# K's features taken to feature rows by transfer instead of by a second transposition

## The chip, the cores and the metric

The kernel runs on one core of a Trainium2 chip. The metric is the device time of one execution in microseconds (us). A change counts here as faster or slower when it moves that time by more than 0.5%, which is about what a measurement of this kernel can tell from no change.

## The reference

Three stages, on inputs with batch 4, 8 heads, 768 positions and 48 features per head. The first is a linear recurrence per head with a complex decay, normalised to a magnitude below one:

```
for t in range(S):
    new_re = ar * S_re - ai * S_im
    new_im = ar * S_im + ai * S_re
    S_re, S_im = new_re + outer(k[t], v[t]), new_im
    y[t] = q[t] @ S_re
```

The heads are then put side by side into x (768 positions of 384 features). The second stage is a token mixer: `theta = x @ w_theta`, `y = w_tok_r @ (x cos theta) + w_tok_i @ (x sin theta)`, `u = x + y`, `u + max(u @ w_ch, 0)`. The third is a gated output: a causal convolution of five taps through a sigmoid gives a gate, and the result is `(gate * (x @ w_val)) @ w_out`.

## The kernel before

The recurrence is computed in chunks of 128 positions. The decay's cumulated logarithm and phase are turned into features: each position's q and k are multiplied by an exponential and by a cosine (tile c) and a sine (tile s), so that 48 features become 96 (a cosine half and a sine half). The score of position t against position t' is then an ordinary product of 96 features.

A granule is 256 positions of one batch, two chunks; there are 12 granules and 24 chunks. For a granule, ScalarE and VectorE make c and s. Their partitions are 16 groups of features times 8 heads, and each partition holds, for each of three features r, 256 words of q features and then 256 words of k features. The matrix products need features on partitions and heads side by side. For q this is done by six transfers per granule, the restacks (lines 616 to 622): one for each of c, s and each r, 128 rows of 256 words, from c or s into the tile st, which has 96 feature rows of 8 heads x 256 positions.

For k a chunk takes another way. TensorE transposes the k words of c and s (trans, line 652, six transpositions), ScalarE evicts them into kn, positions on partitions (kn, line 656, two instructions); TensorE transposes kn once per head, eight transpositions (back, line 660); and ScalarE evicts these into kT, features on partitions (line 663). kT is the stationary operand of the eight score products (line 668), st holds the moving one. kn is needed in any case, as the stationary operand of the state's update (line 699). VectorE masks the scores (line 672), TensorE makes the outputs from masked scores and from the carried state (yT, line 685), ScalarE evicts them (ys, line 688). After each granule the outputs go to memory and TensorE computes theta for them (line 737).

The mixer runs after this attention stage, twelve times, for three groups of 256 positions of each of four batches: the token products (tok, line 852), a first VectorE operation u (line 859), split into high and low parts (lines 792 and 793), a first dense product (line 817, ch), VectorE's o (line 871), four taps of each feature block on VectorE (line 899), a second dense product, the gate, and the output product (line 917). Its weights arrive as 8-byte numbers and are converted by VectorE (lines 419 to 421) and split (lines 489 and 490).

Every piece of work is an operation with a planned engine and duration. The order of all of them is a list written out in the file (ORDER, two characters for the number of an operation); each engine runs its operations in the order in which the list names them, and each of the two queues of transfers, SP's and POOL's, issues in that order. Where the plan sees TensorE idle for over 0.8 us, small dummy products are put in (line 1009). Loads of inputs and weights, restacks and stores are issued by SP; the loads of the mixer and of the input checks by POOL. An issue that waits holds those behind it in its queue.

Buffers: c, s, st, qk and the value tile vt exist twice and alternate by granule, ri three times. Later tiles reuse their places (PLACE): weights of the mixer lie in st0 and st1, which are also the place of kT0 and kT1. Scores, the back transpositions and theta alternate between two tiles of PSUM (A0, A1), in the order of the calls of flip (line 714).

Of the kernel before, what the change touches and what calls it, by code (L numbers as in the profile page):

```python
# [94 lines left out]
class Prog:  # L95
# [10 lines left out]
    ORDER = """  # L106
        #,#.###%#$%9#&I9#)#-#'#0#(%(#*'0#+#/%.%;#2#4%:%=#6#5#9#8#<#7#;#?#:#>#=#1#A#@#D#B#C#G#E#F#J#H#M%?#I%)#K#L$#%@#N$%%A$$'1#[$&$)%B$3$4$'%C$5%*%/
        '2%D#O%+#P#Q#R%<%H#S#U#T#V#Y#W$+#X$1#3#Z$*$($7$0$.$,$>$6%>$/$2$:$<$-$8$D'3$9$@$;'6$B%,$H'7$F%F&H$I%I$?%J$J(;$=%E$K$E$A%-$S$C'8$L$G$Q&I(<%G'9
        $U$M$R$T%0%K%1%M%L$V%N$N%#%O$W%2(A%P%Q$O&T%3%T(B$X&U$P':(C(=$Y%S(>';$Z'?%U%R(D'4'@%V$[%W(J%4%Y'5%['=&&'A'<%X%5&(%Z(E&$&#'>&')I&)%&&*%6&%)J&,
        %7%$&+'B%%&-(K'D&5&.&3%''C&7'E(F&/%8'F)O'J&63A(G&8)P&0)K&93B'G&1(H)Q)L'I&4&:(I)R&2'H&>&;(L)X'K&<'L'Q(N'O&=(O'M&C'R(M)S*X'P'W&?(P'N(R'S'Y*Y(Q  # L110
        )T'U(S&D(?(U'[&A'Z(T(#'X&@&E*Z'T(V()'V($&F(@(+)V(X(W(%&B)#+%(Z(-*[(,(*,*)U(&)+)%+&(.)))W)-)'('(/&G),+'*$(Y(0)$*%)Y)Z([3Q,++()6((+)(1)4)7)[+*
        )&(2)8)*+,++)(*#3R,0).*'*&)M*+,1(3)N)/(4(6*(,,+-)53T(5(7,2,-**&J&V&K)9*,(8+.(9)0*)+/*.+0):(:*2)?,3*0)1*/+1*3,9*1*-);+2*4,4)2*6)<+3+5*:*8*5)3
        ,5+4-8)=*7*;)@*9*<+6-9,6+9*E)>+#*=)B*G*F,7-:)D*>,:+$)C)A)E,8+8-;+7*H)F+:,;)G*?*I+;+>)H+<*C+@+?*@->+D+H+=-?+F*D+A*J+B+I-@+E,>.G+G,<-A*A+C+J*K
        .H,?-B,=-C*N*B,A-D-E-F*L-G,@,C*O+K,.,D*M+S+L*Q*T,/+U*P.I+T,E,B*R*S-H,G-I.J.M,K+V*U,I,F-J*V+M,H.N,L-K+W,Q,J+Q*W,O+N-M-N/R-L,M,S,R-P,P+R+X,U/S
        -O.O,T-S+O-Q,N-R+Y/T-%+P-T.P,V/U-'+Z-&,W-U.V-(-X+[.W.X-<,%.'-Y/X-Z-=&W-V.Q,&.#&X-).(1'-[.R/Y.%-W-#,',#.$/Z1(').S,(.T,X-$.U/[0#.).&,Y-.,$.*.Y
        &L0$.+&M'*1--*-//#.Z.[-0/$,Z-+1.,).4,[1/0%&N-,/(10.5.6.,--.K/%110&-1-41)0'.-.L&Y-3-2120,0-141*&O.2-5&P13-6...315-7/&.7/'./.=.8/)16.90(/*///+
        .0/-/0.:26/,/1/70)/..1/327.;/9/5/80/0*03/:.</V/2.@.C0+/4/;28/6/W0.00.>01/B171802.A.B/D/C29.?1904/@.D.E/<050:2<08.F062=/E/=0>0;1<0B090<2>1;07
        />0@0?/F/A0=1>1B2?0A/G0D/?0C1:2@0M/H1=0K1?2E2A/I1A2C1@1C0E/J1+0N/K/N0F1D1I1,1G0L0O1E/M2F/L2G1M1O2B1J1K1Q1H/O2DB>1F0P1R1N/P1SB;1P0G0Q1L&QB?2K
        &Z/Q&[2#2H0H0V2JB<B@'#2IBA0R0WBEB=0X2%2M&RBB0I0S2$BF2L1Z0J&SBC2P0T2O2N2Q1T0U2:BG0Y0[BH'$2;2W1UBL2R2UBD1#2S0ZBI'%2Y2[2X3C'&3&2V1$3$BM2&'+''1%
        2T1[421V2Z',2'BJ3''-3#BN3D2,1WBO49'.BS3%'(1&BK2(3UBP3F43'/3(3V1X2)4:3G313W443)1Y453HBT2*2-BQ32332.3*463E4;2+5N4@BR4<2/223O3J4=4A3IBW3L4G21BU  # L120
        3KBV203XBZ34233P4&24353+4H3M3/3,BXB[3S3025363Y4$BY3ZC#4'C%C$3-373[C(4%3N6XC&3.4)38C)4#6YC'4(4*C,393:3<474+3;4-3=4,4/C-4>4.C*5A3>486Z404?3?5B
        4B4CC+6[C.5C4DC/4I3@4E4N4JC35D4K7$C0414O4U4L5E5?C15F7%C2C44F7&C64V5G4M7(4PC54Q5H5@7'C:4R5I4S5#4WC74XC;4T7#5$4YC87Y5J4Z5*C<7)7+5K4[5+C9CA5LC=
        5%5M5&7Z5'7,5,5(515-CB5OC>5)5P5Q525T5.CC5U5R58CH5/5W5VC?5X5950C@5S53CD5Y54CI5[7-55CE5:56647.5ZCJ5;CF65CO7/6%CG6#5<CK575=6=CP5>CL6$6>7066CQ6(
        67CMCV71CN6&6'CR6)72686*CW7:6?69736+CS6:6@746,6F6ACX756-6BD$6G7*6C6.768[6;6O6D6<D%8,8$CT6P6/6E608YCU6HD&CY6I8.6177629#D+6J8/786K8-6M6Q796R6L
        8Z6S9%CZ6N6V636T806WD,6U7;819&7[7@7=7A827<7>9,7D8#7C7B7FC[7G7?7ID#7E7J9'D'7H7L9(7K837ND-7MD(8%9-D2847O8;9)7P85D3D)8&7Q868'7R8)7S878(8+92D*94
        8*D4D.7U9.7T93;*D99/D/9$8895;+:'7V7W9+D0D:96D19*7XD589;-97D;:(;.:)908:D@D6;/91:*;1DAD798D88<:,D<8@99:-DB8A8=D=DG9:8>8C8?8F:.8D9;D>8GDH8E;08I
        9<8HD?8K:0DC8L8B:/9=8J9>:3DD8N8MDI9?8ODN:4:+DE8P9A:5DF;(:18QDODJ:68R;):2DP8SDUDK8T<*8UDVDLDM9@<+8VDQ8WDWE#8X<-:79BDR<.9C9GE$:89D9H9EDS:99JE%
        9M</E*9P;,9S<19K::<(DT9N;3E+9FDX<0:;9Q9L<)9OE,9I9RDYE19U9T;29V:BDZ>2E2D[:<9WE&9X>3:=E39YE'E8<,:>9[=/<3:?E9>5;4:@9ZE(=0<2:$E):A>6:#;5E-E::%>7
        =1>8:&E;>9E<;6:CE.=2:D:H;7:E:IE=E/;8E0:K:N:FE4:G:LE>;9:ME?:O<4:QEDE5:R;::P:U=4<5:JEEE6E7=5E@EF:T=6:SEG:V;;:WELEA=8:X;<;C<6EM;=EB<7:YEN;>EO:Z
        ECET=7=3;?EH;#<8=:EU>0;@<9:[EI<:;%EV>1<<=9EWF#EJ;A;$<;EK<=;&EPF$;B?2;'F%EQF&?3F+<>;DERES;FEXF,<?;H;L;O;E?5<@;R;KEYF-?6F.<A;GF3;I?7;NEZ;JE[;Q  # L130
        ;M?9F4F';P?8;T;S;VF5F(;UF6>4<I;WF;<B>:F)?0;XF*<CF<F/>;;Y?1<D;ZF=F>F0<#<EFC<F=;==<%<GF1FDF2=>F7=<FE;[FFF8FK<H<$<&F9FLF:<'F?FM=?<JFNF@<K<OFS=@
        <L<P<M=AFA<RFTFB<S<N<UFG<T=B<WFU<ZFV<QFH=$F[<V<Y=#<XFIG#FJ<[=%FO=C=&=JG$=DG%FP='G*=(=EFQG+FR?4=FFW=)?:=G><G,=H=*G-FX=+G2?;>==I=,FY=-FZG3G&=.
        G4>>=KG5G'G:=P>?=L=M=Q=O=NG;>@=UG(=SG)=XG.=T>A=WG<=VG=?<=YGB>B=ZG/=[>%>C?=GCG0G1>D?>>#G6>$>E>KGD??GEG7>&GJ=RG8GKG9G>>F>'GLGMG?>(GRA0>G?@>)?B
        ?D>HGS?AG@>*GA?CGF>IGTGU>+>,GZGG>J>->.G[GHGI>/GNH#H$?E>LH)>PGO?F>M>Q>NH*>O?G>TGP>SGQ>VGV?H>YH+>UH,>XH1?I>[GW?%>W?#>RAQH2>ZARAP?$GXAO?QGYH3H%
        H4AN?JH9?&H&?'?K?(H:?)?LH'H(H-H;?+H<?MHA?NH.A3@7?-?OHB?*H/@8H0H5?P?,HC?.HDHIH6?/@9?RH7HJ?S?W@:?T?X?VH8@;?Z?UH=@#HK@$HL?[@<@&HQ@)H>@%@=@,@'HR
        @(@+@>H?@*H@@-@FHE@?HSHTHY?YHFHZHGHHHM@@@.H[I#@/I(@AHN@0A6@BI)HO@CA,@2HP@DI*HUI+@1A-@4I0HV@E@3@5I1HW@6HXI$I2A.I3@G@H@LA8A/I%@J@MA;@KA1@P@I@Q
        I&@OI'@T@N@SI,@W@R@Z@UI-@V@X@YA2A<@[AAI.A#I/A4I4A$A5A%I5A&A7A9A'A:A(I6I7A=I8A)A*A?A+A>ABA@AFACAGAHASAIADAEATAXAUAJAYB'AVAZAWALA[B#AKB%B$B&B)
        AMB+B*B(B/B,B-B0B.B1B3B2B5B4B6I:B8I;B9B7B:
    """
# [158 lines left out]
class Kernel:  # L298
# [893 lines left out]
```

## Time and profile before

| | |
|---|---|
| time, median of 3 runs | 544.9 us (543.25 to 546.31) |
| the profiled execution: its own time | 542.7 us |
| its span, first to last instruction | 541.0 us |
| busy: TensorE matmul, weight load, VectorE, ScalarE, GpSimd | 521.0, 476.8, 427.8, 428.1, 91.7 us |
| moved by transfers | 97.70 MB |

PE is TensorE's matmul, PEld its weight load, DVE VectorE, ACT ScalarE, POOL GpSimd, SP the engine that issues most transfers. PEclk is the clock that TensorE was granted, 1.00 being the upper of its two levels. DMA is the mean busy share of the 16 transfer engines. The matmul's ends are modelled, so a busy PE is not a PE at its peak. The stages in time: attention from 0 to about 240 us, the mixer from 240 us to the end.

### The profile page before, as it was taken

What the parts mean: (1) busy time and instruction counts of PE and PEld (TensorE: products, weight loads), DVE (VectorE), ACT (ScalarE), POOL (GpSimd) and SP (SyncE); (2) the same over time, 40 slices, a digit from 0 to 9 for tenths busy, and PEclk for the clock granted to TensorE, in tenths of its full rate; (3) what the DMA queues carried; (4) which work ended last, traced back from release to release, by engine and by line L of the source; (5) the groups of instructions that cost most, each with busy time, mean ns of one, the idle gap of its engine ahead of it and who ended that gap; (6) DMA issues with size and microseconds to landing.
All of it is one profiled execution on the core that took longest, in us unless ns stands there. A gap on an engine that the chain in (4) does not pass through costs nothing.

```text
span 541.0 us, 12968 instructions
## 1 busy us (share of the span) xinstructions
PE 521.0 (96%) x5298; PEld 476.8 (88%) x5298; DVE 427.8 (79%) x589; ACT 428.1 (79%) x790; POOL 91.7 (17%) x185
## 2 busy tenths in 40 slices
PE   8998999999999999999899999999999999999995
PEld 3586797889888898879799999999999999999994
DVE  6999999999999999689899979567683674644552
ACT  7998999999996998986559988778676576664552
POOL 2002000000000011122222233331322222122100
PEclk9999999999999999999899999999999999999998
DMA  8659595867948579748668264453534334233311
GB/s 346 222 182 246 160 294 185 265 210 212 311 166 266 134 196 301 258 147 301 227 216 281 63 205 129 155 179 95 176 118 137 115 101 139 81 118 88 119 44 36
DMA packets 36629, 97.70 MB, mean 181 GB/s; under 512 B 5056, under 2 KB 20432, under 8 KB 36560
## 3 DMA queue, kind: packets, MB, share of 16 engines
q1 hardware_dynamic: 26992, 62.15, 36.5%
q0 software_dynamic: 9568, 34.63, 20.7%
q8 instruction: 43, 0.70, 0.6%
q14 instruction: 26, 0.21, 0.1%
HBM read 73.17 MB, written 14.16 MB: 161 GB/s over the span
## 4 chain that ended last, share of the span: by engine, by line
PE 63%; ACT 14%; DVE 9%; DMA 9%; issue 3%; POOL 0%; SPq 0%; ACTq 0%; POOLq 0%; DVEq 0%
PE A L852 23%; PE A L817 14%; PE Y L917 6%; DMA ri<-in_aT 5%; PE A L668 4%; PE Y L685 4%; PE A L737 4%; ACT L990 2%; PE Y L699 2%; PE A L660 2%; PE X L652 1%; PE X L760 1%; DVE c L604 1%; DMA wraw<-in_wtok 1%; ACT ri L597 1%
## 5 line engine op out<-in xcount | busy, mean ns | idle before, releaser
L899 DVE SCALAR_TENSOR_TENSOR masks<-vt,small,masks 128x256 f32<-128x256 f32 x140 | 60.8, 481 | 2.0 <-ACT masks L882 0.7
L439 ACT ACTIVATE masks<-masks,cst 128x192 f32<-128x192 f32 (+2 forms) x105 | 56.0, 534 | 6.5 <-DMA masks<-in_aT 4.4
L737 PE MATMUL A<-wth,ys 128*128 128x384 f32 x144 | 49.1, 489 | 0.0
L871 DVE SCALAR_TENSOR_TENSOR vt<-A,vt 128x768 f32<-128x768 f32 (+1 forms) x12 | 11.2, 935 | 40.3 <-PE A L817 40.3
L452 POOL DMA_DIRECT2D masks<-in_aT x48 | 26.3, 548 | 87.8 <-ACT masks L439 73.6
L737 PEld LDWEIGHTS A<-wth,ys 128*128 128x128 f32 x144 | 26.3, 190 | 15.6 <-issue 0.2
L817 PE MATMUL A<-st,shch 128*128 128x256 f32 x210 | 32.7, 290 | 3.2 <-ACT st L792 2.3
L685 PE MATMUL Y<-sT,vt 128*32 128x128 f32 x768 | 33.4, 275 | 1.7 <-ACT ys L688 1.0
L431 ACT ACTIVATE masks<-masks 128x192 f32<-128x192 f32 (+1 forms) x57 | 21.1, 369 | 16.3 <-DMA masks<-in_wtok 9.4
L672 DVE TENSOR_TENSOR sT<-A,xt 128x1024 f32<-128x1024 f32 x24 | 29.2, 1217 | 5.7 <-PE A L668 5.5
L817 PE MATMUL A<-sT,kn 128*128 128x256 f32 x210 | 33.3, 284 | 0.0
L817 PEld LDWEIGHTS A<-st,shch 128*128 128x128 f32 x210 | 29.2, 197 | 3.8 <-ACT st L792 2.4
L586 POOL COPY small<-ri 128x3 f32<-128x3 f32 x12 | 5.5, 461 | 158.7 <-DVE ri L577 96.6
L990 ACT ACT_TABLE_LOAD x23 | 29.5, 1283 | 1.2 <-PEq L1181 0.8
L699 PEld LDWEIGHTS Y<-vt,kn 128*96 128x96 f32 x320 | 29.2, 165 | 1.1 <-issue 0.7
L699 PE MATMUL Y<-vt,kn 128*96 128x48 f32 x320 | 30.1, 247 | 0.0
L817 PEld LDWEIGHTS A<-sT,kn 128*128 128x128 f32 x210 | 28.8, 192 | 0.1
L685 PE MATMUL Y<-st,kn 96*32 96x128 f32 x640 | 28.7, 272 | 0.0
L660 PE MATMUL A<-ident,kn 128*96 128x128 f32 x192 | 25.3, 275 | 3.3 <-ACT kn L656 3.3
L917 PE MATMUL Y<-sT,wtmp 128*128 128x384 f32 x120 | 27.1, 339 | 0.0
L660 PEld LDWEIGHTS A<-ident,kn 128*96 128x96 f32 x192 | 20.8, 126 | 6.9 <-ACT kn L656 4.2
L463 POOL DMA_DIRECT2D masks<-in_wtok x32 | 17.2, 537 | 48.0 <-ACT masks L439 24.2
(231 smaller groups left out, 1654.4 us busy)
## 6 DMA issues: line engine op xcount, KB each, us to landing
qk<-in_qkT SPq DMA_DIRECT2D x12, 768.0 KB, 5.9
wraw<-in_wtok SPq DMA_DIRECT2D x12, 768.0 KB, 5.3
masks<-in_aT POOLq DMA_DIRECT2D x48, 192.0 KB, 3.4
ri<-in_aT SPq DMA_DIRECT2D x11, 768.0 KB, 5.7
masks<-in_wtok POOLq DMA_DIRECT2D x32, 192.0 KB, 2.6
vt<-in_v SPq DMA_DIRECT2D x12, 448.0 KB, 4.4
st<-c SPq DMA_DIRECT2D x36, 128.0 KB, 3.8
st<-s SPq DMA_DIRECT2D x36, 128.0 KB, 4.2
```

The source lines that it names most:

```text
L439: self.act(n, lambda: self.nc.scalar.activation(x(), x(), AF.Relu, scale=scale, bias=self.bias(j), accum_out=out()), [b], [b, (self.accb, ...
L452: self.dma("POOL", P * PIECE * 4, lambda x=x, s=src[:, a, c : c + PIECE]: nc.gpsimd.dma_start(x(), s), [], [x], name="ld check")
L660: nc.tensor.transpose(kq()[0:K2, h, :], kn()[:, h].rearrange("p z e -> p (z e)"), self.ident)
L672: self.dve(H * C, lambda: ve.tensor_tensor(sT(), sc(), cm(), op=ALU.mult), [sc, self.causal], [sT], name="mask")
L685: mm(y()[32 * c : 32 * c + 32, blk, :], x[:, at : at + 32], rhs, start=n == 0, stop=n == len(todo) - 1, tile_position=(0, 32 * c))
L699: mm(su()[:, col(h) : col(h) + D], kn()[:, h].rearrange("p z e -> p (z e)"), v(h), start=True, stop=True)
L737: nc.tensor.matmul(th()[:, i, 0:DM], xt()[:, r, i * P : (i + 1) * P], w()[:, r * DM : (r + 1) * DM], start=r == 0, stop=r == R - 1)
L817: nc.tensor.matmul(block(j), w[a]()[:, r * DM + j * P : r * DM + (j + 1) * P], x[c]()[:, r, :], start=first, stop=i == len(todo) - 1 and R ...
L852: nc.tensor.matmul(block(j), z[x]()[:, i, a, j * P : (j + 1) * P], wts[i][y]()[:, o : o + TG], start=first, stop=final)
L899: self.dve(TG, lambda k=k, r=r: ve.scalar_tensor_tensor(gt()[:, r], o()[:, r, k : k + TG], wk(k, r), gt()[:, r], op0=ALU.mult, op1=ALU.add ...
L917: nc.tensor.matmul(ot[i]()[:, 0:DM], gp[a]()[:, r, i * P : (i + 1) * P], w[c]()[:, r * DM : (r + 1) * DM], start=n == 0 and 0 in rs, stop= ...
L990: self.nc.scalar.preload_act_table_set(o)
```

## The change

k's features are restacked together with q's: a restack now moves 128 rows of 512 words (256 of q, then 256 of k), and a row of st is 8 heads x 512 words. The score product takes k from st. The back transpositions, their eviction and the tiles kT0 and kT1 are gone; trans and kn stay. An operation fewer on TensorE and on ScalarE per chunk changes all later numbers, and the list of the order is written anew as a whole: of 2191 numbers 2143 are left. flip is called once less per chunk, so the scores of successive chunks alternate between the two PSUM tiles.

```diff
-    wh10=("c1", 0), ..., ha=("st0", 3072), kT0=("st0", 2048), kT1=("st1", 2048),
+    wh10=("c1", 0), ..., ha=("st0", 3072), 
...
     ORDER = """
...
-        st = self.sb(f"st{p2}", [K2, H, L])
+        st = self.sb(f"st{p2}", [K2, H, 2 * L])
...
-            q.dma_start(rows, x()[:, r, 0:L])
+            q.dma_start(rows, x()[:, r])
...
-                self.dma("SP", P * L * 4, ..., [(x, (0, r))], [(st, (half, r))], name="restack")
+                self.dma("SP", P * 2 * L * 4, ..., [(x, (0, r)), (x, (1, r))], [(st, (half, r))], name="restack")
...
-        k = lambda h: kT()[:, h]
+        k = lambda h: st()[:, h, L + j * C : L + (j + 1) * C]
...
-        kn, kT = self.sb(f"kn{ci % 2}", [P, H, 2, D]), self.sb(f"kT{ci % 2}", [K2, H, C])
-        kq = self.ps(f"A{self.flip()}", [P, H, C])
+        kn = self.sb(f"kn{ci % 2}", [P, H, 2, D])
...
-        def back():
-            for h in range(H):
-                nc.tensor.transpose(kq()[0:K2, h, :], kn()[:, h].rearrange("p z e -> p (z e)"), self.ident)
-
-        self.pe(0.88, back, [kn], [kq], name="back")
-        self.act(H * C, lambda: act(kT(), kq()[0:K2], AF.Copy), [kq], [kT], psum=1, name="kT")
...
-        self.pe(1.79, scores, [st, kT], [sc], name="scores")
+        self.pe(1.79, scores, [st], [sc], name="scores")
```

What the two lists say, read engine by engine with the operations' names: VectorE has 246 operations ahead of the last mask in the old list and 240 in the new. Ahead of the second mix's u it has 314 in both, and they are the same 314 operations. TensorE has, apart from the 24 back groups, the same operations ahead of the second mix's first dense product in both. Between a granule's last feature and the mask of its first chunk the old list has 9 to 26 VectorE operations, the new one 11 to 16 (granules 2 to 12). On SP the new list issues the first load of w_theta ahead of the first load of q and k.

## Rows read from the trace of the kernel before

**Rows 1.** Busy time by stretch: stretch, length, PE, PEld, DVE, ACT, POOL, clock, DMA.

```profile
0.00:20.00 20.00, 18.57 (x73) 7.89 (x74) 14.90 (x43) 16.41 (x37) 2.91 (x13) 1.00 0.86 341
20.00:237.00 217.00, 209.12 (x2731) 179.43 (x2730) 205.65 (x237) 202.58 (x297) 17.19 (x32) 1.00 0.73 221
237.00:287.60 50.60, 47.94 (x556) 45.60 (x554) 44.90 (x64) 33.52 (x63) 10.76 (x19) 0.97 0.70 225
287.60:541.00 253.40, 245.38 (x1942) 243.89 (x1941) 162.33 (x248) 175.59 (x396) 60.86 (x121) 0.99 0.40 124
...
40.00:60.00 20.00, 17.50 (x239) 15.40 (x241) 19.31 (x23) 18.42 (x26) 3.38 (x2) 1.00 0.71 200
60.00:80.00 20.00, 18.35 (x227) 15.53 (x220) 19.05 (x22) 19.93 (x30) 1.39 (x2) 1.00 0.96 263
```

**Rows 2.** Chain of waits, attention stage: start, us, what; first and last of a kind.

```profile
31.33 0.91 ACT st L663
...
137.22 1.01 ACT st L663
...
150.41 1.01 PE A L660 x8
...
224.62 0.87 PE A L660 x8
225.52 2.05 PE A L668 x16
```

**Rows 3.** Who VectorE waited for, 0 to 287.6 us: total, times, longest.

```profile
DVE sT L672 <- PE A L668: 5.5, 5, 4.0
DVE ri L547 <- ACT gt L545: 4.2, 4, 3.0
DVE ri L771 <- ACT ri L768: 2.5, 2, 2.2
DVE c L604 <- ACT ri L597: 1.6, 3, 0.6
DVE st L793 <- ACT st L792: 1.4, 1, 1.4
```

**Rows 4.** Instructions in order of time, start of the second mix: VectorE, then TensorE.

```profile
287.66 0.94 DVE L859 TENSOR_TENSOR vt<-A,ev 128x768 f32<-128x768 f32 x1
...
294.05 0.62 PE L817 MATMUL A<-st,shch 128*128 128x256 f32 x3 [0.59 <-DVE st L793]
```

**Rows 5.** Groups by line: what is removed, back and kT; count, busy, mean ns.

```profile
L660 PE MATMUL A<-ident,kn 128*96 128x128 f32 x192 | 25.3, 275 | 3.3 <-ACT kn L656 3.3
L663 ACT ACTIVATE st<-A 96x1024 f32<-96x1024 f32 x24 | 24.3, 1012 | 0.7 <-PE A L660 0.5
```

**Rows 6.** Transfers, 20 to 237 us: total, then issues, KB each, median us to landing.

```profile
DMA packets 21519, 47.98 MB, mean 221 GB/s; under 512 B 2528, under 2 KB 14304, under 8 KB 21488
...
qk<-in_qkT SPq DMA_DIRECT2D x9, 768.0 KB, 5.4
st<-c SPq DMA_DIRECT2D x36, 128.0 KB, 3.8
st<-s SPq DMA_DIRECT2D x36, 128.0 KB, 4.2
xT<-ys SPq DMA_DIRECT2D x12, 384.0 KB, 4.3
```

**Rows 7.** All restacks (line 618): time from issue to landing.

```profile
DMA to landing us min/median/max: 2.3/4.1/8.7
```

**Rows 8.** Instructions in order of time: SP, TensorE and VectorE, single places.

```profile
2.19 0.43 SPq L520 DMA_DIRECT2D qk<-in_qkT  x1
...
206.49 1.84 SPq L618 DMA_DIRECT2D st<-s  x3
...
5.45 1.09 DVE L547 TENSOR_TENSOR ri<-gt,ri 128x256 f32<-128x256 f32 x3 [3.05 <-ACT gt L545]
...
12.05 1.89 DVE L599 TENSOR_TENSOR s<-s,qk 128x512 f32<-128x512 f32 x3
...
253.94 3.08 PE L1009 MATMUL A<-ident 128*128 128x64 bf16 x100
```

More of the change, by code (lines that the diff above doesn't have):

```diff
@@ L64 @@
     zh0=("qk0", 0), zl0=("qk1", 0), zh1=("gt0", 0), zl1=("gt1", 0),
-    wh10=("c1", 0), wl10=("s1", 0), wh11=("st0", 0), wl11=("st0", 1536), ha=("st0", 3072), kT0=("st0", 2048), kT1=("st1", 2048),
+    wh10=("c1", 0), wl10=("s1", 0), wh11=("st0", 0), wl11=("st0", 1536), ha=("st0", 3072),
     wh20=("st1", 0), wl20=("st1", 1536), la=("st1", 3072), wh21=("c0", 0), wl21=("s0", 0),
@@ L106 @@
     ORDER = """
[L107 to L136, printed above, removed]
@@ L137 @@
-        I&@OI'@T@N@SI,@W@R@Z@UI-@V@X@YA2A<@[AAI.A#I/A4I4A$A5A%I5A&A7A9A'A:A(I6I7A=I8A)A*A?A+A>ABA@AFACAGAHASAIADAEATAXAUAJAYB'AVAZAWALA[B#AKB%B$B&B)
-        AMB+B*B(B/B,B-B0B.B1B3B2B5B4B6I:B8I;B9B7B:
+        #,#.###$#&%5#%#'#*HB#-%$#(#)#0'(#+#/%*%7#2#6%6%9#5#9#4#8#<#7#;#?#:#>#=%%#A#@#D#B#C#G#J%;#E#M#1#F#I#H#K#L%<#N$#%&#[$'%=')$$$%$)$&%'%>$5%?$4%+
+        $3%('*#O%@&@#P%D%8#S#Q#R#V%,#U#T%)#X#W#3#Y$*#Z$0$+$($,$1$6%:$-%E$.$7$<$2%B$/$>'+%F%A$8'.$:$@&A$=%C'/$D$?$A'0%G$E$;'1$9$F'2%-$B$H%I%H(/$G$J%L
@@ new lines @@
+        '3$I%K$C%J$Q%.'4(0$O'5&L$S%M$R'6$K%/$P&M%P$X%N%O$L(1$T'7%Q(2$M'=$U%W$N%S(5'8$Y$V%U%X'9(6'<%T(7%V',':$W%R(8$[%0'-(9';%[%#&$&&$Z'>(:%Y%1(>&#)9
+        '?&'&%(<&(2J'A'B&/%Z'@&-):%2(?);&1%3&0&)'C2K(;&2&.'E)?)<(='G)@&6'I'D(@%4(C(B&*'F'M'Q'O'H'S)A&+'R'K'J&3*D)B'N)C(A'Z'P&,&7(#(D&4(E'['L(F)D*E&8
+        (H(I(3'X&5)H&9&;(4)F(G*F)I(J&:&<)E)J(L*G*J(P(N'T)G&=*K&>(M($(K)M(Q)N(O)K'U(T(X&?(R(Z*L'V(Y(V(U'Y+K*M(%(S*N)(2Z)L(W'W)&)))P)*+L)O)Q)T(&)S*O+M
+        *S([2[)=)U)R('+N)'(((**T*Q)[*U)W*P)Y(+)>+Q*R+R())/3$)V*V*#(,)X)#*X(-)+*&)Z*Y+S*$(.*(*W)$+T,U),*'*Z**)%+U*%)0)-*+*[*)*,)1+V,V*3+%*H+$*1+Z+X*5
@@ new lines @@
+        *-,W*I).+&+#)2*4,X)4+[+,+(+W+**2)5,[*.)3-#+Y+-*:)6+))7-$,&++*6,%+')8-%*/,#*7+2-&+0,$.'+4+3*0+.*;,'*8+5,)+1+6,(-'.(*<+=,,,++O+;*9,**=+/-)*?.)
+        -+,-+P+?+>*@-,+<,3*>--,1-(,/.*.-+7-*..*A./-0,4*B+@-.+8,2.0,0,.+9-1*C.1+A,7,;+:,5.2,=+B,9,<,8-//..3,6-3.4-2,D,:+C,Y-4,B-7+D,E//,F+F.5/0.6-5,Z
+        +G.7&B-6.8,C+E,>-8+H/1.9+I,G&C-:,?-</4-9->+J,@/5.;,K-;/6-B,A-=-D,H/7-@-?-F.<,L08,I-C-G.:/8-E,M.=-H.A-M-A,J.+,N09,P.>0:-N/=/9.?/>,Q.@.,.B,O-I
+        /:,R0;/;.F.C0>-O.D-R-Q.H-P0?-J.N.G.J-V/<.E.L,S.I1C-K-S.O/?/A.K0@.P.M-L-W/B-T/@,T.Q.R&D-X/C&E0A/D1D/E.W/H/20B-U.S-Y0C1E&F/G.X-[0E0G/I/F/3.#.T
@@ new lines @@
+        /K/M0D-Z/J/O.Y.$.U1F1I.%0H0F/Q.[.Z/U1J/#/S0I.V/L0M0L/N/W/$0J/P/X&N.&/%/Y0K&O0N/R0'1K/&0</V/'/)0(0O&G/T1L0S0)0=1M/*0P/(1N0R&H/Z/+0T1R/,0*0Q/[
+        0V/-0X0U0%0Z1O0W0#0Y0&0+1#0[0.1%0$1P1'&P1$1S1)1Q1&&Q&Z0,1+1(1*&[1T1W121X1G1,0/1UAD&I0-1HAG14000103131V&S&JAE1Y1Z022$042#AH1[&T2%1005AF06151-
+        AI2'AKAJ2)072&AN2+1.2(112-2LAL162/231/2*2119&R252,24AM'#AO&KAR172.&U2M'$AP2<184W&V201<1>2='%2>222O1:3BAS&W'&2N1=3%1?&X3;2X3CAQ1;2PATAU261@&Y
+        AY3<2Q1A''3&2:272Y2?3D2;2R3EAV2S2T1B283'2U3(AZ2@3/3#292V3=3-2A3)306(A[3>AW3*3.B'2B3?2C2E3+3F3I6)2W3PAX322D31B#2F333@B(3G3,3J344J353A363Q4K37
@@ new lines @@
+        2G38B)2H4L3KB$396*3L2I4M3HB.3MB%6+3R4N3N3W3:B&4HB/4O3X3SB*6-3T4PB03O4I3U4%B56.4QB+3Y6/3Z4&4R603[3V4#4,6,B64SB,7)B-4-4'4TB14(B74U61B<4)4V7*64
+        4$4*434.B24+B=4/44B340B44X414:B8654Z424Y5#4[5'5$4;5)5*B>455-BC465(B947BD5%484AB:4<5&5+B;4B49BEB?4=BJ5,4>B@66504?5=5/BK4C67BA4D5>BB4E68BLBF4@
+        4F5FBQ4GBG5.5G69525?51BH6:5@6CBI535ABMBR6;625B546<5CBN5H5D5O5I6=BS555JBX5P6>BO565K635L576?BY8+5M5X5E585975BP5N5YBZBT7-5Q6@775R8)5:5;6A8,C&78
+        5S765Z5T6B5[5VBU8.6#8*5W6&5<6$796'6%6DC'7:8/7+6I6F6J7;6E6G6H6L7,856M6K6N6P5U6O6Q6RBV6S806VBW6T7<6U7.B[6W6X7/7=7D816YC#707>866Z717?6[C(7382C-
@@ new lines @@
+        7#727@C$747$8;7%C.C%:3878-8<C)8=847A90C/:47B8>7&83C47'C*7C888991927(:68:C+C5C,8?7E93C0:77I8@7F7J:8C18A7L7HC67O7R::C;8B7N7U957Q7G9694C2C<:97K
+        7M:17TC37P977SC77W:2987V8JC=9:8CC87XCB997Y8D9;C9CC7Z8E;3C:7[C>:5CD8F8$;4:;8G9<8HC?8#CI8&:<9=;1;68I8%;7=;CJC@8'CA;2;8CE;:8(9>8K;9=<8L8P9?CK8Q
+        CF8MCP9@8O8S8U=>8XCG9A=?CQCH8[=@CL8R9%8N8VCR8T8Y=ACW8WCM9#=B8Z9$9BCX9KCNCO9C9&CSCY9'9DD%9(CT9E9)D&CU9FCVCZD'9*9GD,9H;5C[9,:=9I:?D-;;<89+D#;<
+        :>D$D.D(9J<99-9.<:D)D39/:@9LD*<;9M9Q:AD4D+9R9ND/:B9P9T;=9V9Y9S9WD0D5:#9Z9OD:<=9U:&D1:$9XD2D;:C9[D6:%;>:':L:DD<D7DA<>:E;?:(:F<?DB;@:)<<D8:*DC
@@ new lines @@
+        :GD9=9DD<@D=:+:H;A=:DE<B:,:I;B;CD><ADF;E:-:.:J;DD?:/<CD@;FDGDI:0DH:K>;DJDM><DK;G:MDLDNDQ:N;H:O:T:P:UDO:WDP;I:VDR>>:XDU:Y:Q>?;JDS:[DTDV:R>@;K
+        DY;#>A:Z;&:SDW;%DX;$DZ>BE$;';RD[E#E%==;(E(;L=D;)>9E&;*;ME)E'E,=C>:;+;NE*E+<DE-<F;O;-E0;P;,<EE.E/E4;QE1;.;/E5E2E3;0E8<G;SE6E7;XE<<HE9;V;Y;U;T
+        ;W<I;[E=<$E:<'E;<J<#E@<%<(E>E?;Z<+<&ED<*EA<-<)<,EEEB<SEC<K<.EHEF</<LEGEL<0EI<M<1EM<NEJEKEP<3<OENEO=E<P>=EQ<5<Q=GET>C=FER<2>DESEUEX<R<4<6EVEY
+        EW<7F#=HEZ<TE[F$F'<Y=I<V<Z<U<X<W=J=%F(>E=(=$=+=KF%>FF&F)F+F*=L=#F/='=&=M>GF,=)=*=.F0<[>HF-F.F3F1=,F2=-F7=/@9F4=0=T=N=1F8=2F5F6=OF;F9F:=3=P>I
@@ new lines @@
+        F?F<>K>M=Q>JF@=5>NF=>L=RF>FCFA=4FBFG>OFD=6=7FH=SFE=8FFFKFIFJFO>P=UFL=WFP>Q=V>$>#FMFN>&>R=Y>'FS>*FQ=ZFR>S@ZFW>)=XFT>-@W@Y>%=[@[>(@X>+FXFU>.FV
+        >,F[>/FY>T>Z>0FZG&G#>1>U>2G'@<G$>VG%G*>W>3G(>X?@G)>4G+>5G.?A>Y>6G,>7G/G-G2>8G0?BG1>[G3G6?'?C?#?$?(G4?&G7?D?*G5?%?-G:?0?E?+G8?.G9?,G>G;?F?/?2
+        ?3?5?GG<G??1G=?4GB?6?)G@?OGAGFGC?H?7GDGGGE?8?IGJ?9GH?JGIGNGK?;?KGO?L@5?:GL?MGM?=GR?N@6?<GP?>GQGVGS??@7?PGTGWGU?Q?U@8GZ?S?V?R?T@:?YGXG[?XGY?[
+        H%@;@#@&?ZH#@%?WH$H&@(H)@)@$@'@*H'H*H(@J@+@=H-@,H+@>@-H.H,@.@?H1@@@0@B@AH/@CH2H0@DH5@/@2@EH3@F@1H6H4@3H9@H@4@GH7@KH8@I@OH=H:@L@P@QA#@R@M@NA$
@@ L139 @@
+        H>H;A(H<A%@SA)A0A&A*H?A'H@@UA+A,@TA.A-A/A2@VA4A3A1A9HAA6A5A8A7A:A<A;A>A=A?HCAAHDABA@AC
     """
@@ L617, in restack @@
             rows = st().rearrange("f h t -> f (h t)")[half * D + r : half * D + D : R].rearrange("e (h t) -> e h t", h=H)
-            q.dma_start(rows, x()[:, r, 0:L])
+            q.dma_start(rows, x()[:, r])
         for half, x in enumerate((c, s)):
             for r in every:
-                self.dma("SP", P * L * 4, lambda x=x, half=half, r=r: restack(x, half, r, nc.sync), [(x, (0, r))], [(st, (half, r))], name="restack")
+                self.dma("SP", P * 2 * L * 4, lambda x=x, half=half, r=r: restack(x, half, r, nc.sync), [(x, (0, r)), (x, (1, r))], [(st, (half, r))], name="restack")
         ys = self.sb(f"ys{p2}", [P, R, L])
```

## Prediction

> **What bounds the kernel now.** Read first the busy times by stretch [rows 1]. From 20 to 237 us, the attention stage, three engines are nearly full at once: TensorE's matmuls 209.1 of 217 us (96%), VectorE 205.7 (95%), ScalarE 202.6 (93%). After 287.6 us TensorE is alone: 245.4 of 253.4 us, with VectorE at 162.3 (64%). So time won early is worth something only if the second mix begins earlier; from there TensorE runs through to the end. Then the chain of waits [rows 2]: up to about 148 us it goes through ScalarE and VectorE with a few loads, from 148 to 237 us through TensorE almost alone. Of what the change removes, the chain holds ten back groups (150.41 to 224.62 us) and six kT evictions (31.33 to 137.22 us).
>
> The chain ends at one engine at a time and does not say how near the next one is. For that, count what VectorE must do before TensorE can run through. The last time that TensorE waits for VectorE ahead of its run is the second mix's first dense product, at 294.05 us; what it needs begins with VectorE's u at 287.66 us [rows 4]. Ahead of this u stand the same 314 VectorE operations in the old and the new list, and none of them gets shorter. Up to 287.6 us VectorE is busy 14.9 + 205.65 + 44.9 = 265.5 us [rows 1], so idle 22.1 us: 5.1 before 20 us, 11.4 in the attention stage, 5.7 from 237 us on. That idle time, not the removed work, is the purse from which a gain can be paid.
>
> **The change part by part.**
>
> Removed on TensorE: 192 transpositions in 24 groups [rows 5]. A group takes 0.87 to 1.01 us on the chain [rows 2], so 24 x 0.93 = 22.3 us. TensorE keeps 209.1 - 22.3 = 186.8 us of work in the stage.
>
> Removed on ScalarE: 24 evictions of 1.012 us, 24.3 us [rows 5]. ScalarE keeps 178.3 us and is no longer near the bound. The list gives part of this room back to checks and other pieces that can stand anywhere; this I take as nothing, since VectorE doesn't read them.
>
> What VectorE gets from it [rows 3]. It waited 5.5 us for scores, in five waits, the longest 4.0 us, all on TensorE's late products; with 22.3 us less ahead of them I take all 5.5 as gone. It waited 2.5 us for the sine of a rotation, the end of a trip that begins with the last theta on TensorE: gone too, as that theta comes earlier against VectorE's work. It waited 1.6 us for cosines (line 604) and, after the start, 4.2 - 3.0 = 1.2 us for an exponential (line 547; the 3.0 us stand in the start [rows 8]), both ScalarE being late: I take half, 1.4 us. The wait for the parts of the first u (1.4) stays. The idle time of the start, 5.1 us, stays: the new list issues a load of w_theta ahead of the first q and k, whose 768 KB are issued at 2.19 us and, at 5.4 us to land [rows 6, 8], are there at 7.6 us; even 2.5 us later they come before their use at 12.05 us [rows 8]. Sum: 5.5 + 2.5 + 1.4 = 9.4 us. The ceiling is the 22.1 us less the start and some 3 us of gaps of a few ns between instructions: 14 us.
>
> Added on the transfers: 72 restacks x 128 KB = 9.4 MB on the 48.0 MB that the stage moves [rows 6]. At present 221 GB/s go with a busy share of 0.73 [rows 1], so a full share moves 303 GB/s; 57.4 MB in a stage of 209 us are 275 GB/s, a share of 0.91. Throughput is there, but little is over. For the trip of one restack the trace has no row of 256 KB between tiles; the nearest are 128 KB in 3.8 to 4.2 us and a store of 384 KB in 4.3 us [rows 6], so the lower end is no growth at all (in these rows no larger transfer lands sooner, which excludes a gain), and the upper is a doubling to 8.4 us, near the longest of today, 8.7 [rows 7]. I take 128 KB at the full share's rate, 0.43 us each; the three of a half follow each other in 1.84 us [rows 8], so the last of them is 3 x 0.43 = 1.3 us later. The number of issues on SP and their 0.6 us each stay. The trip from the last feature to the mask is 1.84 + 4.2 + 2.0 (scores [rows 2]) = 8.0 us today and 9.3 us after; between the last feature and the granule's first mask VectorE has at least 9 operations in the old list and 11 in the new one, at a mean of 205.65 / 237 = 0.87 us [rows 1], and today's masks waited in 5 of 24 cases only. I take the added 1.3 us as covered in all granules but one: 1.3 us lost.
>
> The Trainium skill, Perfetto Trace Analysis, section Identifying the Most-Contended Engine, says to judge TensorE by its weight loads and not by its busy matmuls, and to work on the engine of the highest occupancy. In the attention stage the weight loads are busy 179.4 of 217 us (83%) against VectorE's 205.7 (95%) [rows 1]. By that rule the change relieves the wrong engine and can pay only out of VectorE's idle time; by the matmul row, 96%, the groups on the chain would be won in full, which is the first rival below. The trace bears the rule out before 148 us, where the chain leaves TensorE, and less after.
>
> Also added: room on TensorE. Dummy products are put into planned gaps, now 100 in one gap taking 3.1 us [rows 8]; more planned gaps bring more of them, in time that TensorE doesn't need, so nothing. Nor do I charge the clock: TensorE's share of the stage falls to 186.8 of 209, 89%, and from 40 to 60 us it is at 17.5 of 20 (87.5%) with a clock of 1.00 [rows 1].
>
> Freed otherwise: the scores no longer wait for trans, kn, back and kT in turn, and no longer share their PSUM tiles with back. That loosens TensorE's order, which the item of 5.5 us already holds.
>
> **Sum.** 9.4 - 1.3 = 8.1 us, taken as 8. After the second mix's first dense product both lists hold the same TensorE work, so 8 us go through to the end: span 541.0 to 533, the execution's own 542.7 to 534.7. The median shown is 544.9, 2.2 above that execution, so 536.9: 537 us.
>
> **The rivals.**
>
> First, TensorE and ScalarE set the pace as the chain has it: ten back groups x 0.93 = 9.3 us, plus the six kT pieces on it, 0.56 to 1.01 us each, 4.9 us together [rows 2]: 14.2 us, 530.7 us. For it speaks that 148 to 237 us is TensorE without a break. Against it, that VectorE would then have to work to within its ceiling of 14 us, every wait gone and none new. 13%.
>
> Second, hidden anyway: VectorE's waits for scores are replaced by waits for restacks, or the rotation's trip stays late behind fuller transfers, and the gain is under 2.7 us: 543 to 546, say 544 us. For it, VectorE at 95% of the stage and a transfer share going to 0.91. Against it, 22 us of slack that TensorE and ScalarE gain behind them. 16%.
>
> Third, slower: the restacks become the bound. The place is VectorE's mask (line 672) of a granule's first chunk, which then waits for scores that wait for the last of six restacks queued behind loads of 768 KB. Every us by which the trip grows beyond its cover is lost once per granule. It decides from 8.1 / 11 = 0.74 us per granule; at 1.5 us uncovered in each of 11 granules it takes 16.5 us and leaves the time at 544.9 + 16.5 - 9.4 = 552 us. For it, a share of 0.96 already stands from 60 to 80 us [rows 1] and the longest restack took 8.7 us [rows 7]. Against it, loads are issued two granules ahead, and the cover has held in 19 of 24 masks. 11%.
>
> **How the numbers follow.** The forecast has 60%: its own range, from the ceiling and from the restacks' share, is 531 to 542. The first rival lies at its edge, at 530.7, and with a few us from a new order late in the mixer it reaches 529; the second is held to 545, the third lies outside. Range 529 to 545, leaving out about 2 in 10. Within 0.5% of 544.9 is 542.2 to 547.6. Faster: 60 + 13 = 73%. Same: 16%. Slower: 11%.
>
> **What would show it.** Right: VectorE's wait for line 668 under 2 us, its idle time ahead of the second mix's u down from 22 to about 14 us, that u at about 280 us, weight loads in the stage down by about 20 us; ScalarE below 90%; TensorE visibly idle in the attention stage, and the restacks landing in 4 to 5 us. Wrong: VectorE waits for scores of over 10 us in many short waits (third rival); u of the second mix before 275 us (first) or after 285 us (second); or TensorE idle after 300 us, which would mean that the shift is not carried to the end. A granted clock under 0.95 between 40 and 220 us would be an error of its own.

## The result: slower, by the transfers

The changed kernel takes 552.7 us (median of 20 runs, 544.3 to 563.3) against 543.6 us before (20 runs, 541.1 to 547.2). The ratio is 1.011, 95% interval 1.0085 to 1.0136. It takes the runs within 1.5% of each kernel's fastest, ten of the 20 here and all 20 before, so it gives a smaller loss (6.0 us) than the medians (9.1 us). The profiled execution took 557.1 us, 14.4 us more than that of the kernel before, so the rows below show more loss than either; why the changed kernel's runs scatter by 19 us is not shown. Its span is 554.9 us. The forecast was 537 us.

Busy time by stretch in the changed kernel (columns as in [rows 1]), cut at the second mix's u; below the line two stretches of 20 us:

```profile
0.00:20.00 20.00, 18.57 (x78) 8.07 (x79) 14.66 (x42) 16.37 (x36) 2.73 (x13) 1.00 0.87 341
20.00:237.00 217.00, 195.54 (x2396) 162.95 (x2394) 190.17 (x223) 173.50 (x252) 29.36 (x24) 0.94 0.94 248
237.00:301.60 64.60, 60.52 (x796) 56.87 (x796) 57.66 (x79) 43.47 (x79) 13.77 (x24) 0.94 0.67 224
301.60:554.90 253.30, 245.37 (x1942) 243.62 (x1940) 161.80 (x248) 179.05 (x404) 63.88 (x125) 0.99 0.42 126
...
40.00:60.00 20.00, 15.49 (x160) 13.10 (x157) 15.81 (x19) 15.49 (x23) 7.80 (x2) 0.83 1.03 261
80.00:100.00 20.00, 15.46 (x175) 13.05 (x167) 15.61 (x18) 14.97 (x21) 1.34 (x3) 0.83 0.92 252
```

From 20 to 237 us the three engines that were nearly full are less busy than in [rows 1], TensorE by 13.6 us, VectorE by 15.5, ScalarE by 29.1; the transfers are fuller, 0.94 against 0.73. VectorE is busy 262.5 us ahead of the second mix's u (265.5 before), so it is idle 39.1 us there instead of 22.1: the purse did not shrink to 14 us but grew. The u itself, from the instructions in order of time:

```profile
301.58 0.95 DVE L851 TENSOR_TENSOR vt<-A,ev 128x768 f32<-128x768 f32 x1
```

It comes 13.9 us later than in [rows 4], and the span ends 13.9 us later. The last row by stretch and that of [rows 1] are equal: 253.3 and 253.4 us from u to the end. All of the loss is made ahead of this u, and most of it in the attention stage: the last mask starts at 241.1 us, 9.7 us later than before (231.4).

Who VectorE waited for up to 300 us (total, times, longest), to be read against [rows 3]:

```profile
DVE sT L664 <- PE A L660: 14.0, 9, 4.0
DVE gt L561 <- ACT gt L554: 6.4, 4, 4.2
DVE kn L701 <- PE Y L691: 4.6, 2, 3.7
```

And a piece of the chain of waits (start, us, what), which answers to [rows 2]:

```profile
195.41 1.76 DVE s L603
...
197.77 0.60 SPq L617
...
198.41 8.41 DMA st<-s
...
207.06 3.75 PE A L660 x16
210.82 5.31 PE A L729 x12
```

The wait for scores, 5.5 us before and forecast to vanish, is 14.0 us, and behind it stands a restack: feature, issue, 8.4 us of transfer, then scores. For the last 4.0 us of the transfer TensorE has nothing to do. The granted clock is then at 0.50, its lower level, from 207 to 213 us, and one chunk's scores take 3.75 us where one chunk's took 2.05 us [rows 2] before. Over the whole execution TensorE is idle for 16.6 us just before score products, where it was 1.1 us before. The profile names a restack for 7.8 of them (group by line: busy us, mean ns, idle us before):

```profile
L660 PE MATMUL A<-st 96*128 96x128 f32 x384 | 56.1, 310 | 16.6 <-DMA st<-s 7.8
```

So the delay goes through TensorE first. VectorE's masks of the first chunks, which scores behind restacks hold up directly, waited 4.6 us in all, as much as before; the other 9.4 us are masks of second chunks, whose scores TensorE reaches late (both read from the masks in order of time). e7 below, with the same bytes to the same rows, shows the same: 17.2 us idle before scores, 9.3 of them for a restack, and 17.0 us of VectorE's wait.

The transfers of the whole execution (first row: queue, packets, MB, share of 16 engines' span; then as in [rows 6]):

```profile
q1 hardware_dynamic: 26992, 71.59, 45.3%
...
st<-c SPq DMA_DIRECT2D x36, 256.0 KB, 7.6
st<-s SPq DMA_DIRECT2D x36, 256.0 KB, 7.2
```

All restacks together, as in [rows 7]:

```profile
DMA to landing us min/median/max: 3.2/7.4/12.4
```

The queue in the kernel before:

```profile
q1 hardware_dynamic: 26992, 62.15, 36.5%
```

In time of all 16 engines that is 0.453 x 554.9 = 251.4 us against 0.365 x 541.0 = 197.5 us: 9.4 MB more cost 54 us, not the 31 us that 303 GB/s would make. (It is the sum of the packets' times, and these overlap where a share is above 1, as below; it compares kernels and is not a busy time of the engines.) The two stretches below, of the changed kernel (columns of [rows 1]), show why. In the first, four us in which the restacks of the chain above are under way, the engines are full and move 138 GB/s; in the second, with the loads that follow, they are as full and move 373 GB/s.

```profile
197.00:201.00 4.00, 4.00 (x84) 3.64 (x75) 4.00 (x8) 2.18 (x5) 0.00 (x0) 1.00 1.11 138
...
205.00:207.00 2.00, 0.00 (x0) 0.00 (x0) 1.97 (x3) 1.98 (x3) 0.52 (x1) 0.94 0.98 373
```

The kernel before shows the same while its restacks run; this row could have been read before the prediction:

```profile
190.00:192.00 2.00, 2.00 (x18) 1.82 (x17) 1.79 (x4) 2.00 (x4) 1.07 (x2) 1.00 1.14 158
```

### The profile page after: what moved, and what is told of

Same layout as the page of the kernel before. It is cut to its first block, busy times and chain, and to the rows that moved or that the text cites. A ratio compares the mean times of both kernels' runs of the same rounds, so it can differ in the third digit from the quotient of the medians.

```text
span 554.9 us, 12757 instructions
## 1 busy us (share of the span) xinstructions
PE 520.0 (94%) x5205; PEld 471.5 (85%) x5205; DVE 424.3 (76%) x589; ACT 412.4 (74%) x768; POOL 109.7 (20%) x185
## 4 chain that ended last, share of the span: by engine, by line
PE 56%; DMA 10%; DVE 6%; ACT 5%; issue 5%; SPq 1%; POOL 0%; ACTq 0%; DVEq 0%; POOLq 0%
PE A L844 21%; PE A L809 12%; PE Y L909 6%; DMA st<-s 5%; PE A L660 5%; PE A L729 4%; PE Y L677 3%; PE Y L691 2%; SPq L617 1%; DMA st<-c 1%; DMA wraw<-in_wout 1%; PE X L752 1%; DMA wraw<-in_wtok 1%; DMA qk<-in_qkT 1%; PE X L650 1%
## 5 line engine op out<-in xcount | busy, mean ns | idle before, releaser
L660 PE MATMUL A<-st 96*128 96x128 f32 x384 | 56.1, 310 | 16.6 <-DMA st<-s 7.8
L660 PEld LDWEIGHTS A<-st 96*128 96x128 f32 x384 | 53.3, 222 | 19.6 <-issue 17.3
L438 ACT ACTIVATE masks<-masks,cst 128x192 f32<-128x192 f32 (+1 forms) x105 | 56.1, 534 | 4.2 <-DMA masks<-in_aT 2.0
L729 PE MATMUL A<-wth,ys 128*128 128x384 f32 x144 | 52.6, 514 | 0.0
L585 POOL COPY small<-ri 128x3 f32<-128x3 f32 x12 | 23.3, 1943 | 140.7 <-DVE ri L576 77.8
L729 PEld LDWEIGHTS A<-wth,ys 128*128 128x128 f32 x144 | 28.1, 204 | 16.9 <-issue 3.3
L809 PE MATMUL A<-st,shch 128*128 128x256 f32 x210 | 31.5, 283 | 1.4 <-ACT st L784 1.0
L691 PE MATMUL Y<-vt,kn 128*96 128x48 f32 x320 | 31.5, 253 | 0.0
L462 POOL DMA_DIRECT2D masks<-in_wtok x32 | 17.2, 537 | 54.0 <-ACT masks L438 38.6
L979 PE MATMUL X<-ident 128*128 128x512 bf16 x111 | 26.1, 400 | 1.4 <-POOL ident masks.py:199 1.4
## 6 DMA issues: line engine op xcount, KB each, us to landing
st<-c SPq DMA_DIRECT2D x36, 256.0 KB, 7.6
st<-s SPq DMA_DIRECT2D x36, 256.0 KB, 7.2
```

The costliest lines, as they stand in the source:

```text
L438: self.act(n, lambda: self.nc.scalar.activation(x(), x(), AF.Relu, scale=scale, bias=self.bias(j), accum_out=out()), [b], [b, (self.accb, ...
L660: mm(sc()[:, h, :], k(h), q(h), start=True, stop=True)
L691: mm(su()[:, col(h) : col(h) + D], kn()[:, h].rearrange("p z e -> p (z e)"), v(h), start=True, stop=True)
L729: nc.tensor.matmul(th()[:, i, 0:DM], xt()[:, r, i * P : (i + 1) * P], w()[:, r * DM : (r + 1) * DM], start=r == 0, stop=r == R - 1)
L809: nc.tensor.matmul(block(j), w[a]()[:, r * DM + j * P : r * DM + (j + 1) * P], x[c]()[:, r, :], start=first, stop=i == len(todo) - 1 and R ...
L979: self.nc.tensor.matmul(self.kp()[:, 1, :].rearrange("p (a b) -> p a b", a=2), x[:, 0:P], x.rearrange("p (o b) -> p o b", o=1).to_broadcas ...
```

## The experiments

Times are medians; each ratio is to the kernel before on the same chip, with its 95% interval. "Queue" is q1's share times the span of the one profiled execution, the time that SP's transfers took of all 16 engines. There are 20 runs of the changed kernel, 2 of e8 and 4 to 11 of the others. The experiments ran on four chips; differences between two experiments are therefore taken between their ratios, times 543.6 us.

| kernel | us | ratio | queue, us |
|---|---|---|---|
| before | 543.6 | 1 | 197.5 |
| changed | 552.7 | 1.011 (1.0085 to 1.0136) | 251.4 |
| e1, before + bytes | 589.1 | 1.074 (1.066 to 1.082) | 260.9 |
| e2, changed without bytes | 536.4 | 0.983 (0.979 to 0.988) | 189.5 |
| e3, changed, old list | 578.1 | 1.062 (1.055 to 1.068) | 255.6 |
| e4, changed, rows spread | 537.7 | 0.988 (0.984 to 0.992) | 224.8 |
| e5, before, rows spread | 543.8 | 1.002 (0.999 to 1.006) | 189.6 |
| e6, e1 with rows spread | 568.7 | 1.048 (1.044 to 1.051) | 233.4 |
| e7, changed, two pieces | 557.2 | 1.026 (1.019 to 1.032) | 256.0 |
| e8, changed, rows adjacent | 596.0 | 1.098 (1.089 to 1.107) | 296.4 |
| e9, changed, every eighth row | 549.0 | 1.008 (1.005 to 1.011) | 231.8 |
| e10, e3 with rows spread | 561.9 | 1.032 (1.028 to 1.037) | 232.3 |
| e11, bytes that nobody reads | 548.4 | 1.011 (1.006 to 1.015) | 236.8 |

**e1.** The kernel before, restacks of 512 words, rows of st as long as in the change, kT kept (in a place of its own).

```diff
-            q.dma_start(rows, x()[:, r, 0:L])
+            q.dma_start(rows, x()[:, r])
```

> The kernel before with its own order, its back transpositions and their eviction, but with restacks of 512 words: k's half is moved and nothing reads it. Theory T (the added bytes are dear: in the changed kernel the engines move only 123 to 156 GB/s at a full share while restacks flow, and the transfers' total grew by 54 us): clearly slower than before, by 2% to 4% (555 to 566 us), since all the work that the change removes is still there; the restacks land in 7 to 8 us. Theory O (the newly written order is what costs): within 0.5% of before, about 544 us.

Measured 589.1 us, ratio 1.074: the bytes alone cost 40 us in the old list (45 us by the medians), more than expected. The restacks land in 8.8 us (median), above the 7 to 8 us expected. VectorE's wait for scores is 28.9 us there:

```profile
DVE sT L672 <- PE A L668: 28.9, 12, 5.7
```

**e2.** The changed kernel with q's halves alone.

```diff
-            q.dma_start(rows, x()[:, r])
+            q.dma_start(rows, x()[:, r, 0:L])
-        k = lambda h: st()[:, h, L + j * C : L + (j + 1) * C]
+        k = lambda h: st()[:, h, j * C : (j + 1) * C]
```

> The changed kernel with its new order, but restacks of 256 words as before; the scores take q's rows in place of k's as the stationary operand, so k is left out of the scores. Theory T: without the added bytes the removal pays what the prediction's sum gives it before the restacks, 8 to 10 us: 534 to 536 us against 543.6, and the granted clock back at 0.99. Theory O: stays slower than before, about 550 us.

536.4 us, 0.983. The removal with its new list pays 9.0 us (0.0166 x 543.6; 6.5 to 11.5 by the interval), near the prediction's sum before the restacks, 9.4 us. Theory O falls. The granted clock did not come back to 0.99 as expected; it lies at 0.983 to 0.986 in three executions and at 0.968 in the fourth, the profiled one.

**e3.** The changed kernel, the list of before with its 48 removed numbers struck out (no other edit).

> The changed kernel with the list of before, the 48 removed operations struck out of it and nothing else moved. Theory T: about as slow as the changed kernel, 550 to 558 us, since the same bytes flow. Theory O: the old order with less work is at or below before, 536 to 544 us.

578.1 us, ratio 1.062, worse than both theories said. From kernel to kernel, by the ratios: the bytes in the old list +40 us (e1), the removal there -7 (e3 less e1; their intervals overlap a little), the new list -27 (changed less e3), which leaves the +6 us of the change. The new list was not the cost; it gave most of the cost back.

**e4.** The changed kernel, feature rows in another order: one restack writes every sixth of 96 rows instead of every third of 48. The selection matrix and kn follow.

```diff
-            rows = ...[half * D + r : half * D + D : R]...
+            rows = ...[half * R + r : K2 : 2 * R]...
-            act(kn()[:, :, z].rearrange("p h (e r) -> p h e r", r=R), ...
+            act(kn()....rearrange("p h (e z r) -> p z h e r", z=2, r=R)[:, z], ...
```

> The changed kernel with its order and bytes, but feature rows laid out so that one restack writes every sixth of 96 rows (both halves interleaved) instead of every third of 48. Theory T1 (the restack is slow because its 16 destination rows lie close together and share ways into the memory): landings fall from 7.4 to under 6 us, the transfers' busy total falls by 20 us or more, and the time to 540 to 547 us. Theory T2 (the restack is slow by its bytes or by its kind, tile to tile, wherever it writes): unchanged, 550 to 555 us.

537.7 us, 0.988, under both kernels and under the 540 to 547 us of theory T1, with the same bytes, the same list and the same operations. Its restacks' landing:

```profile
DMA to landing us min/median/max: 3.1/4.8/9.5
```

VectorE's wait for scores up to 280 us:

```profile
DVE sT L664 <- PE A L660: 3.1, 4, 1.3
```

And its second u, in order of time:

```profile
284.02 0.95 DVE L851 TENSOR_TENSOR vt<-A,ev 128x768 f32<-128x768 f32 x1
```

The u comes 3.6 us sooner than before and the span, 537.7 us, is 3.3 us shorter. The restacks of the granule shown above for the changed kernel, in the same four us of their course:

```profile
191.00:195.00 4.00, 4.00 (x80) 3.63 (x76) 4.00 (x8) 2.18 (x5) 0.00 (x0) 1.00 1.08 223
```

That is 223 GB/s where the changed kernel moved 138, at about the same share. Of theory T1 this shows that where the rows lie decides; that rows share ways into the memory is its explanation, and no run shows it directly.

**e5 and e6.** The same edit in the kernel before, and in e1.

> The kernel before, bytes and order unchanged, with the rows of features spread over 96 as in e4. Theory T1 (close destination rows slow each restack): landings fall below 3.8 us, but the transfers were not what bounded this kernel, so the time stays within 0.5%, 541 to 545 us. Rival: the transfers bounded the kernel before as well, and it gains over 1%, below 538 us.

> e1 (the kernel before with restacks of 512 words, k's half read by nobody) with rows spread over 96. Theory T1: most of e1's 45 us go away, to 550 to 565 us; what is left over before is the price of the bytes themselves. Theory T2 (the bytes are dear wherever they go): stays at 580 to 592 us, and e4's gain came from something else in the layout.

e5 is 1.002, no difference, with landings of 3.5 us: the queue falls by 8 us, but there the transfers had room. e6 gives back 14 of e1's 40 us (20 of 45 by the medians), less than expected; the other 26 us are the price of the bytes in the old list even where rows are spread.

**e7.** Each restack as two transfers of 256 words.

```diff
-            q.dma_start(rows, x()[:, r])
+            for a in range(2):
+                q.dma_start(rows[:, :, a * L : (a + 1) * L], x()[:, r, a * L : (a + 1) * L])
```

> The changed kernel with each restack issued as two transfers, 256 words of q and 256 words of k, so packets of 1 KB as before the change and the same bytes to the same rows; 72 more issues of 0.6 us on SP. Theory S (rows of 2 KB are slow, 1 KB is not): transfers' total falls by 15 us or more and the time to 540 to 548 us. Theory T1: the rows are the same, so the time stays at 548 to 558 us, or worse by the added issues.

557.2 us and a queue of 256.0 us: the length of a row is not it, theory S falls. By the ratios it is 8 us above the changed kernel: cutting the restacks, with 72 more issues, costs time of its own.

**e8.** The 16 rows of a restack side by side (`half * D + 16 * r` and the 15 after it; the selection matrix and kn follow).

> The changed kernel with the 16 rows that a restack writes put side by side (the opposite of e4). Theory T1: closer rows are slower, landings above 9 us and the time above 570 us. Theory T2 or S: as the changed kernel, 548 to 558 us.

596.0 us. Its restacks' landing:

```profile
DMA to landing us min/median/max: 4.4/8.8/16.7
```

With e4 this makes a scale: adjacent, every third, every sixth row take 296, 251, 225 us of the queue and 596, 553, 538 us. The time follows; the median landing (8.8) stayed under the 9 us that was expected.

**e9.** Six of every eight rows of 128, the other rows cleared at the start.

```diff
-            rows = ...[half * D + r : half * D + D : R]...
+            rows = ...[half * R + r : K2 : 8]...      # K2 = 128
```

> The changed kernel with its order and bytes; features lie in every eighth row of 128 (six of eight rows used, the others cleared once at the start), so that a restack's 16 rows stand 8 apart. Theory T1, that rows within some distance of each other share a way: if that distance is 8 rows, no two of the 16 meet, landings fall below e4's 4.8 us, the transfers' hardware queue falls below e4's 41.8% of the span, and the time is 533 to 537 us, under both kernels. If rows as far as 8 apart still share, or the pacing is elsewhere: as e4, 537 to 539 us.

549.0 us: no further gain; the queue (231.8 us) and the median landing (5.9 us) are above e4's. So it isn't the distance between rows alone, and these runs don't settle which rows share a way. Part of the time has another cause: the clearing holds up the start. In its first 20 us (columns of [rows 1]) POOL is busy 11.4 us and VectorE gets 33 instructions done instead of the changed kernel's 42:

```profile
0.00:20.00 20.00, 18.57 (x80) 8.15 (x81) 15.04 (x33) 13.68 (x30) 11.43 (x16) 1.00 0.81 307
```

**e10.** e3 with e4's rows.

> e3 (the removed operations struck out of the old list) with rows spread over 96. If the restack's longer trip is all that hurts e3, it comes from 578 us down to e4's 537 to 541 us; if the old list itself, made for a shorter trip, costs too, it stays at 545 to 560 us.

561.9 us, a little above the second case's span: the old list costs 24 us against e4 at the same bytes and rows. What in it costs (its uneven cover of 9 to 26 VectorE operations ahead of a mask would fit) was not tested.

**e11.** A granule's six q halves first, then its six k halves, which nobody reads.

```diff
-            q.dma_start(rows, x()[:, r])
+        later = []
...
+            q.dma_start(rows[:, :, 0:L], x()[:, r, 0:L])
+            later.append((rows[:, :, L : 2 * L], x()[:, r, L : 2 * L]))
+            if len(later) == 6:
+                for d, y in later:
+                    q.dma_start(d, y)
-        k = lambda h: st()[:, h, L + j * C : L + (j + 1) * C]
+        k = lambda h: st()[:, h, j * C : (j + 1) * C]
```

> The changed kernel with its order; a granule's six q halves are restacked first, then its six k halves to the same rows, and nobody reads the k halves: the scores take q's rows as the stationary operand, so k is left out of them (as in e2). All bytes of the change flow, with 72 more issues on SP, but no product waits for the added ones. Theory A (what hurts is the longer trip of what the scores wait for): 534 to 541 us, as e2. Theory B (what hurts is the fullness of the transfer engines, for every load and store alike): 546 to 556 us, as the changed kernel.

548.4 us, inside theory B. By the ratios e11 is 15 us above e2 and level with the changed kernel, although no score waits for the added bytes. Not all of it is fullness, as the 72 added issues of SP are in it; e7, which has them too, is 8 us above the changed kernel. And e7, where the scores wait for the same pieces, is 8 us above e11. If these parts simply add up, which was not tested, then of the 15 us between e2 and the changed kernel about 7 are full transfer engines and 8 the scores' wait for the added bytes, each uncertain by several us. So both probably count. One sign of the fullness is the load of q and k: it lands in 5.9 us (median) before, 6.4 in e2, 8.1 in e11 and 8.6 in the changed kernel.

## Why the prediction was wrong

**The step that failed** is "I take 128 KB at the full share's rate, 0.43 us each", and with it "covered in all granules but one: 1.3 us lost". The 303 GB/s were a mean over all transfers of the stage, most of them loads (373 GB/s in the stretch above). The restacks ran at 138 to 158 GB/s. The added bytes took 54 us of the engines instead of 31, the median landing went from 4.1 to 7.4 us, near the upper bound that I had named (8.4) and not priced into the range, the way from a granule's last feature to its last restack's landing grew by 3.1 us (6.6 to 9.7, median of granules 2 to 12) and not by 1.3, and the share of 0.91 that I called enough became 0.94 for the stage and 1.03 from 40 to 60 us.

**The rival that came true** is the third, at 11%: priced at 552 us, measured 552.7. That the restacks would become the bound is right; that the price met the median is luck. It was made of 1.5 us lost at the first mask of each of 11 granules. Those masks waited 4.6 us in all, no longer than before; the time was lost on TensorE ahead of the scores (16.6 us idle, then the lower clock) and came to VectorE at second chunks and elsewhere. And by e11 bytes which no score waits for probably cost time too, beyond its added issues; the rival did not have this.

**Held as a total:** what the removal pays. The sum was 9.4 us, e2 gives 9.0. The Trainium skill, Perfetto Trace Analysis, section Identifying the Most-Contended Engine, had led to VectorE instead of TensorE; e2 agrees as far as that the chain's 14.2 us of the first rival were not reached (11.5 at the end of its interval). That the second mix's u decides held in every trace looked at for it: from u to the end 253.4 us before, 253.3 after, 253.7 in e4.

**Not shown, and partly against it:** the terms of that sum. e2's one trace is of an execution of 543.5 us, which shows no gain, and has 6.1 us of waits for scores where none were forecast. In e4, whose trace has a gain, they are 3.1 us, a longer wait for an exponential stands beside them (5.1 us, 0.2 before), and the purse did not shrink:

```profile
0.00:20.00 20.00, 18.57 (x75) 7.96 (x76) 14.82 (x44) 16.49 (x37) 2.99 (x13) 1.00 0.87 342
20.00:237.00 217.00, 204.23 (x2591) 168.88 (x2589) 203.48 (x238) 188.94 (x270) 31.68 (x29) 0.98 0.86 262
237.00:284.02 47.02, 43.23 (x604) 42.28 (x603) 43.88 (x64) 30.78 (x60) 11.02 (x19) 1.00 0.73 241
```

VectorE is busy 14.8 + 203.5 + 43.9 = 262.2 us ahead of u, so idle 21.8 us, as in the kernel before (22.1). The u comes sooner because VectorE's busy time is 3.3 us shorter for the same operations, a term that the prediction put at nothing ("none of them gets shorter"). The durations add up to 285.5 us against 286.1; the rest is that successive ones overlap by 23.3 us in all instead of 20.6. Why is not shown.

**The forecast's number without its reason:** e4 reaches 537.7 us with the whole change in place, once the restack is cheaper. Since the idle time did not fall, its nearness to 537 us is luck as far as the trace goes.

**Wrong beside it:** the clock. I charged nothing for it, arguing from a stretch at 87.5% busy and 1.00 [rows 1]. In the changed kernel it is 0.83 from 40 to 60 and from 80 to 100 us: the idle time did not come evenly, but in waits of several us (4.0 us for the restack above). The restacks are not the whole cause, as e2, without the added bytes, has 0.983 to 0.986 at best where the kernel before has 0.986 to 0.998 on the same chip. What the clock cost by itself was not measured; in the scores alone TensorE is busy 56.1 us in the changed kernel, 48.3 before.

The Trainium skill, DMA: Bandwidth & Descriptors, section Where 436 GB/s comes from, puts the ceiling of transfers between tiles at 435 GB/s, the fabric's. The measured rate of this restack, 138 GB/s at full engines, is a third of that, and here the measurement decides.

## What to carry to other kernels

Price added bytes at the rate of the transfer that carries them, read in a stretch where it alone is under way, not at the mean rate of the stage. When work moves from engines to transfers, write the transfers' share beside the engines' as one more bound, and where it comes near full, as in this stage (0.94), expect other loads to be late, not only the transfer that grew. In a transfer between tiles that gathers many partitions into few, try other destination rows before giving it up: e4 changed the layout alone and turned 1.1% slower into 1.2% faster.

## What had not been expected of the hardware

The rate of a transfer between tiles depends on which partitions it writes: with 16 rows of 16 KB each, adjacent, every third and every sixth took 296, 251 and 225 us of the queue for the same bytes. Every eighth of 128 rows took 232 us, so more distance is not always better; these runs don't settle the rule behind it.
